# The first batch of a channel-attention and gated feed-forward kernel: ten groups of squares added up on VectorE, all norm products behind the scores, four filler products in place of fifty-six

## The chip, the cores and the metric

The kernel runs on one core of one Trainium2 chip. The metric is the device time of one execution in microseconds, over several executions of each kernel.

A profile shows one execution. PE is TensorE, PEld its weight loads, DVE VectorE, ACT ScalarE, POOL GpSimd.

## The reference, cut to what matters

```python
def _attn_ref(q, k, v, tau):                      # (4, 6016, 256) each
    qn = q / (np.linalg.norm(q, axis=1, keepdims=True) + 1e-06)
    kn = k / (np.linalg.norm(k, axis=1, keepdims=True) + 1e-06)
    s = kn.transpose(0, 2, 1) @ qn / tau          # 256 x 256 per batch
    a = softmax(s, axis=-1)                       # cut: written out with max, exp, sum
    return v @ a
def _moe_ref(x, w_gate, w_val, w_out):            # x: the attention's rows, d_ff 1536
    return (sigmoid(x @ w_gate) * (x @ w_val)) @ w_out
```

The norm runs over all 6016 rows, so nothing of a batch's attention can be finished before its last rows of q and k are there.

## The kernel before

The kernel folds `a` into the feed-forward weights, so the main loop multiplies v by folded weights (`gh_G`, `gh_H`) and then by `w_out`. For batches 1 to 3 the scores and norms are side work in the loop of the batch before. For batch 0 they stand in front of everything: the prologue. It works on groups of 4 x 128 rows, the last group being cut in two (groups 11 and 12).

```python
def score(b, t0, u):                 # per 128 rows: 2 products into the 256 x 256 scores
    ...
def squares(b, t0, nt, which, engine, sq=None):   # elementwise squares, q on VectorE, k on ScalarE
    # (the last group the other way round)
    ...
def norm_mms(ps, sqs, nt, first, last, order=(0, 1)):
    for w in order:                  # column sums of the squares: one product per 128 columns
        for u in range(nt):
            for j in range(CB):
                mm(ps[:, w*CB+j : w*CB+j+1], sqs[w][:, u, ds(j*P, P)], ones_bf[:, 0:1], ...)
def busy(n):                         # filler products that keep TensorE at work
    ps = psg.tile([P, CH], FP32, tag="g", name="ps_busy")
    for _ in range(n):
        mm(ps, ones_bf, ones_wide, True, True)    # 512 wide

busy(9)
n_acc = NT // TPC - 2                # 9 groups are added up on VectorE into acc
for g, (t0, nt) in enumerate(groups0):
    # squares; if 0 < g < n_acc: acc += sq (two additions on VectorE)
    # scores of the group
    if g < n_acc:          busy(5)
    elif g == n_acc:       norm_mms(acc); norm_mms(sq of group 9)
    elif nt == TPC:        busy(2); norm_mms(sq of group 10)
    elif g < last0:        held = (sq, nt)
    else:                  norm_mms(held); norm_mms(sq of group 12)
norms_sqrt(0)                        # ScalarE, then the table load for exp
...                                  # invert, spread, weights (exp), folded weights gh(0, 0..4)
```

## Time and profile before

| | before |
|---|---|
| median time | 830.18 us (829.69 to 830.32, 3 runs); 829.94 us with 3 more |
| span of the profiled execution | 827.9 us |
| PE busy | 817.6 us (99%) |
| first product of the main loop (ps_gate) | at 39.08 us |
| last k tile used by scores / square root of the norms / first weight product | 33.5 / 34.32 / 36.85 us |

From 40 us on, TensorE has almost no idle time (busy 19.95 of the 20 us to 60 us, and 739.3 of the 740 us from 60 to 800 us), so the end moves only if the first ps_gate product moves. In the timeline, a line gives start, length, engine, source line, operation and count. The bracket says how long the engine was idle before the line and what ended that.

### The profile page before, as it was taken

To read this page: it belongs to the slowest core of one execution; us is meant where nothing else is said; L and a number is where in the kernel's file an instruction comes from. 1 tells how busy PE (TensorE), PEld (TensorE's weight loads), DVE (VectorE), ACT (ScalarE), POOL (GpSimd) and SP (SyncE) were. 2 spreads that over 40 slices of the span, in tenths; PEclk is the share of its full clock that TensorE was granted. 3 is DMA by queue.
4 is the path that set the end of the run, shared out by engine and by line. 5 is a ranking of instruction groups with operands and counts; after the bars stand their busy time and mean duration, and the time that the engine had idled before them with its cause. 6 is when DMAs were issued, how large, how long until landed. Compare 5 with 4: busy or idle time off the path is not lost.

```text
span 827.9 us, 13794 instructions
## 1 busy us (share of the span) xinstructions
PE 817.6 (99%) x5204; PEld 503.5 (61%) x5218; DVE 588.7 (71%) x1023; ACT 391.7 (47%) x644; POOL 83.1 (10%) x159
## 2 busy tenths in 40 slices
PE   8899999999999999999999999999999999999998
PEld 4556666665665666665575666666566566666666
DVE  6577877787667777778767777777766666666665
ACT  4654444446644444445654444444655444444442
POOL 5532100002110100000311010000000000000000
PEclk9999999999999999999999999999999999999999
DMA  9999623226846433233875352223323423322111
GB/s 210 206 202 212 112 52 90 59 54 136 154 93 118 96 89 61 53 52 87 155 139 128 81 106 57 51 64 74 64 62 63 71 52 86 68 49 70 45 36 72
DMA packets 79027, 77.19 MB, mean 93 GB/s; under 512 B 50800, under 2 KB 55920, under 8 KB 78960
## 3 DMA queue, kind: packets, MB, share of 16 engines
q0 software_dynamic: 23920, 38.81, 28.1%
q1 hardware_dynamic: 54752, 36.91, 17.6%
q8 instruction: 41, 0.67, 0.3%
q10 hardware_dynamic: 288, 0.59, 0.2%
q14 instruction: 26, 0.21, 0.1%
HBM read 78.64 MB, written 24.64 MB: 125 GB/s over the span
## 4 chain that ended last, share of the span: by engine, by line
PE 94%; DMA 4%; DVE 1%; issue 0%; POOL 0%; ACT 0%; POOLq 0%
PE ps_o L88 30%; PE ps_gate L88 29%; PE ps_val L88 29%; PE ps_s L88 4%; DMA q_sb<-in_q_dram 3%; PE ps_gh L88 2%; DMA w_val<-in_moe_w_val_dram 1%; DVE hT L424 0%; DVE sq L176 0%; PE ps_end L88 0%; ACT g_sb L423 0%; PE ps_n L88 0%; POOL k_sb L97 0%; POOL q_sb L97 0%; PE ps_tp L394 0%
## 5 line engine op out<-in xcount | busy, mean ns | idle before, releaser
L424 DVE TENSOR_TENSOR hT<-ps_val,g_sb 128x512 bf16<-128x512 f32 (+1 forms) x576 | 390.7, 679 | 205.6 <-ACT g_sb L423 201.0
L423 ACT ACTIVATE g_sb<-ps_gate 128x512 bf16<-128x512 f32 (+1 forms) x576 | 338.3, 588 | 386.0 <-PE ps_gate L88 379.7
L88 PE MATMUL ps_gate<-vT,gh_G 128*128 128x512 bf16 (+1 forms) x1152 | 337.7, 375 | 0.2
L88 PE MATMUL ps_val<-vT,gh_H 128*128 128x512 bf16 (+1 forms) x1152 | 337.5, 375 | 0.3
L88 PE MATMUL ps_o<-w_out_sb,hT 128*128 128x256 bf16 x2244 | 324.9, 273 | 0.0
L88 PEld LDWEIGHTS <-hT 128*128 128x128 bf16 x2268 | 221.0, 98 | 124.6
L88 PEld LDWEIGHTS <-gh_H 128*128 128x128 bf16 x1152 | 112.7, 98 | 131.6 <-issue 1.0
L88 PEld LDWEIGHTS <-gh_G 128*128 128x128 bf16 x1152 | 112.4, 98 | 37.8 <-DVE gh_G L379 0.4
L106 POOL DMA_DIRECT2D v_sb<-in_v_dram x48 | 25.6, 533 | 619.7 <-DMA vT<-v_sb 498.5
L450 DVE COPY out_sb<-ps_o 128x256 f32<-128x256 f32 x187 | 77.2, 413 | 12.6 <-PE ps_o L88 12.6
L88 PE MATMUL ps_s<-k_sb,q_sb 128*128 128x256 bf16 x376 | 67.0, 276 | 3.9 <-DMA k_sb<-in_k_dram 2.7
L88 PEld LDWEIGHTS <-q_sb 128*128 128x128 bf16 x376 | 37.1, 99 | 12.7 <-issue 5.0
L215 DVE TENSOR_TENSOR acc<-acc,sq 128x1024 bf16<-128x1024 bf16 (+1 forms) x66 | 44.1, 669 | 0.0
L176 DVE TENSOR_TENSOR sq<-q_sb 128x1024 bf16<-128x1024 bf16 (+2 forms) x44 | 29.3, 667 | 2.7 <-DMA q_sb<-in_q_dram 2.7
L97 POOL DMA_DIRECT2D k_sb<-in_k_dram x48 | 26.2, 545 | 17.1 <-DMA k_sb<-in_k_dram 8.1
L97 POOL DMA_DIRECT2D q_sb<-in_q_dram x48 | 26.3, 548 | 14.9 <-DMA q_sb<-in_q_dram 7.4
L176 DVE TENSOR_TENSOR sq<-k_sb 128x1024 bf16<-128x1024 bf16 (+2 forms) x34 | 22.4, 658 | 0.9 <-ACT sq L174 0.9
L88 PE MATMUL ps_busy<-ones_wide,ones_bf 128*128 128x512 bf16 x57 | 17.7, 440 | 1.7 <-DVE shift L127 1.6
L174 ACT ACTIVATE sq<-k_sb 128x1024 bf16<-128x1024 bf16 (+1 forms) x11 | 11.2, 1018 | 14.5 <-DMA k_sb<-in_k_dram 13.1
L487 DVE TENSOR_TENSOR acc<-acc,sq 128x1024 bf16<-128x1024 bf16 x16 | 11.1, 691 | 5.5 <-ACT sq L174 5.2
L88 PE MATMUL ps_gh<-w_val,e_sb 128*128 128x512 bf16 x44 | 13.4, 379 | 0.2
L88 PEld LDWEIGHTS <-e_sb 128*128 128x128 bf16 x112 | 10.2, 98 | 4.7 <-ACT e_sb L311 0.5
(67 smaller groups left out, 133.8 us busy)
## 6 DMA issues: line engine op xcount, KB each, us to landing
out_dram<-out_sb SPq DMA_DIRECT2D x44, 512.0 KB, 2.9
v_sb<-in_v_dram POOLq DMA_DIRECT2D x44, 256.0 KB, 3.8
q_sb<-in_q_dram POOLq DMA_DIRECT2D x43, 256.0 KB, 7.3
k_sb<-in_k_dram POOLq DMA_DIRECT2D x43, 256.0 KB, 8.0
out_dram<-out_sb SPq DMA_DIRECT2D x3, 384.0 KB, 2.5
w_gate<-in_moe_w_gate_dram POOLq DMA_DIRECT2D x3, 256.0 KB, 6.8
w_val<-in_moe_w_val_dram POOLq DMA_DIRECT2D x3, 256.0 KB, 7.4
w_out_sb<-in_moe_w_out_dram POOLq DMA_DIRECT2D x1, 768.0 KB, 12.7
```

What stands on the lines that cost most here:

```text
L88: nc.tensor.matmul(out, lhsT=lhsT, rhs=rhs, start=start, stop=stop, **kw)
L97: nc.gpsimd.dma_start(out=tl[:, :nt, :], in_=rows(src, b)[:, t0 : t0 + nt, :])
L106: nc.gpsimd.dma_start(out=v_sb[:, :nt, :], in_=rows(v, b)[:, t0 : t0 + nt, :])
L174: nc.scalar.activation(out=sq[:, :nt, :], in_=src[:, :nt, :], func=ACT.Square)
L176: engine.tensor_tensor(out=sq[:, :nt, :], in0=src[:, :nt, :], in1=src[:, :nt, :], op=ALU.mult)
L215: nc.vector.tensor_tensor(out=acc[:, :nt, :], in0=acc[:, :nt, :], in1=st[b]["sq", w][:, :nt, :], op=ALU.add)
L423: nc.scalar.activation(out=g_sb[:, :n], in_=ps_gate[:, :n], func=ACT.Sigmoid)
L424: nc.vector.tensor_tensor(out=hts[b, ci][:, f, :n], in0=ps_val[:, :n], in1=g_sb[:, :n], op=ALU.mult)
L450: nc.vector.tensor_copy(out=out_sb[:, s, :], in_=ps)
L487: nc.vector.tensor_tensor(out=acc[w], in0=acc[w], in1=sq[w], op=ALU.add)
```

## The change

Its intent is to spend less TensorE work on the prologue. VectorE adds up one more group (60 norm products become 44), all norm products stand behind the last score, and 4 fillers remain of 56 (a few later ones stay as they are). In both diffs and code, `...` marks a cut.

```diff
-    sqpool = pool("sqpool", 2)
+    sqpool = pool("sqpool", 3)
...
-    busy(9)
-    n_acc = NT // TPC - 2
+    n_acc = NT // TPC - 1
+    parts = [(acc, TPC)]
     for g, (t0, nt) in enumerate(groups0):
...
+        elif g:
+            parts.append((sq, nt))
         for u in range(nt):
             score(0, t0, u)
-        if g < n_acc:
-            busy(5)
-        elif g == n_acc:
-            norm_mms(ps_n0, acc, TPC, True, False)
-            norm_mms(ps_n0, sq, nt, False, False)
-        elif nt == TPC:
-            busy(2)
-            norm_mms(ps_n0, sq, nt, False, False)
-        elif g < last0:
-            held = (sq, nt)
-        else:
-            norm_mms(ps_n0, *held, False, False)
-            norm_mms(ps_n0, sq, nt, False, True, (1, 0))
+        if n_acc - 3 <= g <= n_acc:
+            busy(1)
+    for n, (sq, nt) in enumerate(parts):
+        norm_mms(ps_n0, sq, nt, n == 0, n == len(parts) - 1, (1, 0) if n else (0, 1))
```

## The prediction

> **What bounds the kernel now.** I read the page first, then the chain in order of time for 26 to 41 us, then the timeline of the first 40 us. The change touches only the first batch's scores and norms, so the first question is what share of the span that is.
>
> ```profile
> span 827.9 us, 13794 instructions
> PE 817.6 (99%) x5204; PEld 503.5 (61%) x5218; DVE 588.7 (71%) x1023; ACT 391.7 (47%) x644; POOL 83.1 (10%) x159
> ```
>
> TensorE is busy for 99% of the span. The three big product groups (ps_gate, ps_val, ps_o) carry 88% of the chain, and the change touches none of them. Its only field is the prologue, about 39 us, before the first ps_gate product at 39.08. What bounds the prologue is in the chain:
>
> ```profile
> 19.61 10.58 DMA q_sb<-in_q_dram
> 30.19 0.28 issue
> 30.47 6.80 DMA w_val<-in_moe_w_val_dram
> 37.27 0.04 issue
> 37.31 0.59 PE ps_gh L88 x2
> ```
>
> From 3.46 to 37.27 us (start, length, what) nearly the whole chain is transfers: the loads of q and k, queued one after the other, then the first w_val tile. TensorE work there is not on it. The stretches say the same (PE, PEld, DVE, ACT, POOL busy, clock, DMA share, GB/s):
>
> ```profile
> 20.00:26.00 6.00, 4.73 (x28) 2.69 (x28) 4.92 (x8) 2.11 (x2) 2.25 (x5) 1.00 1.13 211
> 26.00:32.00 6.00, 4.44 (x58) 3.38 (x58) 2.28 (x4) 2.59 (x3) 2.75 (x5) 1.00 1.16 203
> ```
>
> The DMA share is above 1 and 203 to 211 GB/s flow, while PE has gaps. But one line of work runs beside the w_val transfer and ends almost with it. From the timeline:
>
> ```profile
> 33.19 0.82 PE L88 MATMUL ps_s<-k_sb,q_sb 128*128 128x256 bf16 x6
> 33.84 0.44 PE L88 MATMUL ps_n<-ones_bf,sq 128*128 128x1 bf16 x12
> 34.32 0.17 ACT L278 ACTIVATE r<-ps_n 128x4 f32<-128x4 f32 x1 [0.50 <-PE ps_n L88]
> 34.51 1.28 ACT L505 ACT_TABLE_LOAD   x1
> 35.88 1.65 ACT L311 ACTIVATE e_sb<-y_sb,shift,r 128x128 bf16<-128x128 f32 x4
> 36.85 0.38 PE L88 MATMUL ps_gh<-w_gate,e_sb 128*128 128x512 bf16 x1
> ```
>
> Read downwards: last scores, last 12 norm products, square root, table load, exponentials, first weight product at 36.85. That one holds PE for two 512-wide products of 0.215 us, so to 37.28; the next needs w_val, which landed at 37.27. So the **slack of the norm line is only about 0.03 us**: transfer and norm line end together. Whatever lengthens the norm line moves the end.
>
> [...] (1) [...]the 12 norm products start at 33.84 and the filler behind them at 34.15, 26 ns each; 16 from 32.79 to 33.19 are 25 ns each. (2) [...]512-wide fillers are 0.43 us apart up to 10.11 us, and 0.215 us apart later; 8 scores take 1.86 us at 6.74 and 1.03 us at 12.58. The profile's clock column shows 1.00 throughout, so this state has to be read from spacings. (3) [...]The trace has 1.28 us; [...]the exponential starts 0.09 us after the load. (4) [...]GpSimd's load issues take 0.53 us whether or not a VectorE product lies over them (12.14 us and 10.83 us), so more additions should not hold back the loads.
>
> **The change, part by part.**
>
> *Fillers.* The program issued 9 at the start, 5 after each of nine groups and 2 at group 10: 56. Four remain (groups 7 to 10). At 0.215 us each, 52 x 0.215 = 11 us of PE work goes (more, as the early ones ran at 0.43). Before about 33 us all of it lies beside transfers: from 22 us on, PE waits for k each time (idle of 0.42 to 1.21 us before scores). **Worth 0 us**, except that PE no longer lags behind arrivals before 20 us, which it had caught up with by then anyway.
>
> *One more group added up on VectorE.* Group 9 gets two additions of 0.691 us (the 16 present ones took 11.1 us). VectorE was busy 2.28 of 6.00 us from 26 to 32. The second addition follows ScalarE's square, which ends at 29.06 + 1.06 = 30.12, so it runs to 30.81; the q square of group 10 slips from 30.28 to 30.81 and ends at 31.50, before its k square (31.52 to 32.58). **Worth 0 us.** It saves 16 norm products: 60 become 44.
>
> *Three buffers for squares.* The squares of groups 10, 11 and 12 now all live until the end. With three buffers none waits. **0 us.**
>
> *Norm products behind the scores.* This is the part that costs. Before, 16 (acc) and 16 (group 9) ran in a gap near 29.9, 16 more at 32.79 before the scores of group 11, and only 12 stood behind the last score. Now all 44 stand there. The gain: the k of group 11 is in at about 32.89 (ScalarE's square starts), so its 4 scores no longer wait until 33.19; but group 12's 2 scores need its last k, in at about 33.46 (issued 26.96, 6.5 us to landing). So the scores are through at about 33.76, not 33.84: 0.08 us gained. The loss: 44 - 12 = 32 more products x 25.6 ns = 0.82 us. The last square is done at 33.82 and is multiplied last, so it adds nothing. Net: the square root starts 0.82 - 0.08 = **0.74 us later**.
>
> *Behind that.* The table load is queued after the square root, the exponentials after the load, so all of it shifts by 0.74 us. The copies of the scores on VectorE no longer matter, and the fillers in front of ps_rk run meanwhile. The first weight product goes from 36.85 to 37.59; w_val is then long in. After the 0.03 us of slack, **about +0.7 us** remains. Nothing later takes it back, as PE has hardly any idle time after 40 us (15.95 of 16 us busy from 44 to 60).
>
> Sum with the array at full rate at the end of the prologue: 830.18 + 0.7 = 830.9 us.
>
> **The rivals.** *A cold array.* With the fillers gone, PE starts cold at 6.74. Cold, 8 scores last about 1.7 us of a 2.5 us group period (68%). For: the kernel before only got fast after 10.11 us, although PE was busy from 1.60 with one gap of 1.14 us[...]. Warm, only 0.87 of 2.5 us is busy (35%), 1.09 with the filler. Against: groups 0 to 2 run nearly without a gap from 6.74 to about 12.3 when cold[...]; gaps afterwards are 1.5 us[...]; and the four fillers raise a cold array to 85% just before the end. If it is cold at 33 us: 6 scores + 0.4 us, 44 norm products perhaps + 1.1, the four fillers and ps_rk about + 1, the first weight products + 1; about 3.5 us on top, so 834.5 us. I give this one chance in four, some of it in milder form.
>
> *Hidden after all or a gain.* If the norm line had slack that I misread (w_val landing later in most runs than in the profiled one), the 0.7 us would be hidden: 830.2. If the earlier scores or the idler PE gained anything, it is at most a few tenths, as transfers set the pace: 829.9. One chance in six together.
>
> *VectorE or the loads slowed.* More additions holding up load issues would move every later landing. The trace speaks against it (4). One in twenty; about + 1 us.
>
> **Range and chances.** The likeliest value is 830.9, the cold tail pulls the median up a little: 831.1. Low end 829.9 (a small gain, near the fastest runs before), high end 834.2 (most of the cold case). 2% is 16.6 us; the whole prologue is 39 us and bound by transfers, so neither bound is in reach.
>
> **What would show it.** Right: the row of ps_n shows 44 products in one block of about 1.1 us starting near 33.8; the square root starts near 35.1; the first ps_gate near 39.8; the q, k and w_val landings unchanged within a few tenths; all after 40 us merely shifted. Cold: 8 scores near 1.7 us at groups 9 and 10, ps_gh products 0.43 us apart. Wrong: a square root that starts no later than 34.4, w_val landing later than 37.6, or a loop after 40 us that itself changed length.

0.82 - 0.08 - 0.03 is about +0.7 us, on 830.18 us, so 830.9 us. In (3), the 1.28 us are those of the table load. The rival of a cold array (834.5 us) is the estimate from the two rates in the trace of before; at how much work or idle time the rate changes was not shown.

## The result, and the profile after

The changed kernel takes 829.73 us (829.49 to 829.80, 6 runs), against 829.94 us (829.69 to 830.32, 6 runs) for the kernel before. The ratio is 0.9997 with a 95% interval of 0.9984 to 1.001: **the same**. Ratios here are the mean time of one kernel's fast runs over that of the other's of the same rounds, so they are not quite the ratio of the medians quoted. The forecast class was right. The forecast number was not: 829.73 lies just below the stated low end of 829.9, and the forecast direction (+0.7 us) did not come.

The page of the changed kernel, its busy row and the granted TensorE clock in 40 slices:

```profile
span 827.8 us, 13658 instructions
PE 810.3 (98%) x5138; PEld 500.3 (60%) x5150; DVE 590.4 (71%) x1025; ACT 391.7 (47%) x644; POOL 83.4 (10%) x159
PEclk8799999999999999999999999999999999999999
```

TensorE does 7.3 us less work and the span is the same (827.8 against 827.9 us), because that work stood beside transfers. The clock row begins with 8 and 7, so the array now runs at a lower rate in part of the prologue. ("Cold" below means at half rate: granted clock 0.50, 8 scores in 1.86 to 1.87 us. "Warm" means at full rate: 1.00, and 1.03 us.) By stretch (PE, PEld, DVE, ACT, POOL busy, then granted clock, DMA share, GB/s):

```profile
14.00:20.00 6.00, 3.68 (x20) 2.38 (x19) 4.43 (x7) 2.55 (x3) 2.42 (x6) 0.68 1.12 209
20.00:26.00 6.00, 4.10 (x19) 2.54 (x19) 4.92 (x9) 2.17 (x3) 2.53 (x5) 0.50 1.12 209
26.00:33.00 7.00, 6.02 (x32) 3.75 (x32) 4.31 (x8) 3.84 (x5) 4.32 (x7) 0.73 1.17 205
```

From 16.1 to 29.8 us the array was at half rate, and the transfers flowed as before (205 to 209 GB/s; 206 to 211 before, in the same stretches). The cold array cost nothing, as it was warm again before the last k (32.86 us). The end of the prologue in the timeline after, the same rows as the prediction shows of before:

```profile
32.23 1.05 PE L88 MATMUL ps_s<-k_sb,q_sb 128*128 128x256 bf16 x6
...
33.12 0.54 PE L88 MATMUL ps_n<-ones_bf,acc 128*128 128x1 bf16 x16
...
33.52 0.84 PE L88 MATMUL ps_n<-ones_bf,sq 128*128 128x1 bf16 x28
...
34.40 0.17 ACT L278 ACTIVATE r<-ps_n 128x4 f32<-128x4 f32 x1 [1.19 <-PE ps_n L88]
...
34.59 1.28 ACT L499 ACT_TABLE_LOAD   x1
...
36.92 0.38 PE L88 MATMUL ps_gh<-w_gate,e_sb 128*128 128x512 bf16 x1
```

The longer norm line is there. From the first product behind the last score to the square root it takes 34.40 - 33.12 = 1.28 us, against 34.32 - 33.84 = 0.48 us before: 0.80 us more, where 0.82 was predicted. But it **begins 0.72 us earlier**, at 33.12 rather than 33.84, where 0.08 was predicted. So the square root comes 0.08 us later (34.40: the prediction had named "no later than 34.4" as a sign of being wrong), and the first ps_gate at 39.13 instead of 39.08. The chain after confirms that the norm line is now on it, behind the last k:

```profile
26.38 6.48 DMA k_sb<-in_k_dram
32.87 0.04 issue
32.91 0.38 PE ps_s L88 x2
33.28 1.08 PE ps_n L88 x44
34.36 0.24 PE ps_busy L88
```

The last k is in at 26.38 + 6.48 = 32.86 us. Before, by its issue at 26.96 and 6.5 us to landing, it was in at about 33.46. Where does that 0.6 us come from? GpSimd's issues, which wait for earlier loads to land, show it. Before:

```profile
23.39 0.53 POOL L97 DMA_DIRECT2D k_sb<-in_k_dram  x1 [0.70 <-DMA k_sb<-in_k_dram]
24.89 0.53 POOL L97 DMA_DIRECT2D q_sb<-in_q_dram  x1 [0.97 <-DMA q_sb<-in_q_dram]
26.96 0.53 POOL L97 DMA_DIRECT2D k_sb<-in_k_dram  x1 [1.54 <-DMA k_sb<-in_k_dram]
28.03 0.53 POOL L106 DMA_DIRECT2D v_sb<-in_v_dram  x1 [0.54 <-DMA q_sb<-in_q_dram]
```

After:

```profile
23.66 0.53 POOL L97 DMA_DIRECT2D k_sb<-in_k_dram  x1 [0.70 <-DMA k_sb<-in_k_dram]
25.16 0.53 POOL L97 DMA_DIRECT2D q_sb<-in_q_dram  x1 [0.97 <-DMA q_sb<-in_q_dram]
26.38 0.53 POOL L97 DMA_DIRECT2D k_sb<-in_k_dram  x1 [0.69 <-DMA k_sb<-in_k_dram]
27.44 0.53 POOL L106 DMA_DIRECT2D v_sb<-in_v_dram  x1 [0.52 <-DMA q_sb<-in_q_dram]
```

One wait differs: 1.54 us instead of 0.69, a load that landed 0.85 us late in the kernel before. Everything else runs at the same pace; the changed kernel had been 0.27 us behind until then (23.66 against 23.39), which leaves the 0.58 us. The DMA view of that moment (24 to 25 us of before; queue, packets, MB, share of the 16 transfer engines) has a second queue in it:

```profile
q0 software_dynamic: 102, 0.19, 103.6%
q8 instruction: 1, 0.02, 6.1%
```

In the changed kernel the first such packet is at 34.5 us (34 to 35 us):

```profile
q0 software_dynamic: 203, 0.19, 118.0%
q8 instruction: 1, 0.02, 5.8%
```

The view names the kind of this queue "instruction", so I read its packets as fetches of instructions. The one at 24.1 us took 0.97 us (6.1% of 16 engines for 1 us), the one at 34.5 us 0.94 us. Each has 16,384 bytes, and the DMA view counts 41 of them (0.67 MB) before and 40 (0.66 MB) after. So the **theory**, mine and tested below: a change in the number of TensorE's instructions moves the packet in time. With 52 fillers and 16 norm products fewer (the page counts 5,138 products and 5,150 weight loads, against 5,204 and 5,218 before) it comes 10.4 us later, behind the last k instead of in front of it, and that gave back what the norm line cost.

The packet is not gone. At 34.5 us the w_val tiles are still on their way, and now they are late. The view of w_val gives the time from issue to landing of its three loads, before and then after:

```profile
DMA to landing us min/median/max: 6.8/7.4/8.7
DMA to landing us min/median/max: 7.3/8.0/9.1
```

The first of them is the shortest. It was issued 0.58 us earlier than before (29.89, not 30.47) and landed at 37.2 us, as before (37.27). In the traces of all thirteen profiles it landed between 37.1 and 37.5 us: in 6.8 us where no packet fell between its issue and its landing, in 7.3 to 7.6 us where one did. So moving the packet behind k shortens the norm line, but not the line through w_val.

### The profile page after: what moved, and what is told of

Same layout as the page of the kernel before. It is cut to its first block, busy times and chain, and to the rows that moved or that the text cites. A ratio compares the mean times of both kernels' runs of the same rounds, so it can differ in the third digit from the quotient of the medians.

```text
span 827.8 us, 13658 instructions
## 1 busy us (share of the span) xinstructions
PE 810.3 (98%) x5138; PEld 500.3 (60%) x5150; DVE 590.4 (71%) x1025; ACT 391.7 (47%) x644; POOL 83.4 (10%) x159
## 4 chain that ended last, share of the span: by engine, by line
PE 95%; DMA 3%; POOL 1%; DVE 1%; issue 0%; ACT 0%; POOLq 0%
PE ps_o L88 30%; PE ps_gate L88 29%; PE ps_val L88 29%; PE ps_s L88 4%; DMA k_sb<-in_k_dram 3%; PE ps_gh L88 2%; DVE hT L424 0%; POOL q_sb L97 0%; PE ps_n L88 0%; POOL k_sb L97 0%; DVE sq L176 0%; PE ps_end L88 0%; ACT g_sb L423 0%; ACT e_sb L311 0%; PE ps_busy L88 0%
## 5 line engine op out<-in xcount | busy, mean ns | idle before, releaser
L106 POOL DMA_DIRECT2D v_sb<-in_v_dram x48 | 25.6, 533 | 620.5 <-DMA vT<-v_sb 487.5
L88 PE MATMUL ps_s<-k_sb,q_sb 128*128 128x256 bf16 x376 | 73.1, 298 | 13.2 <-ACT k_sb L130 7.0
L88 PEld LDWEIGHTS <-q_sb 128*128 128x128 bf16 x376 | 40.0, 106 | 23.6 <-issue 8.9
L88 PE MATMUL ps_gh<-w_gate,e_sb 128*128 128x512 bf16 x41 | 12.8, 379 | 0.2
```

The source lines that it names most:

```text
L88: nc.tensor.matmul(out, lhsT=lhsT, rhs=rhs, start=start, stop=stop, **kw)
L106: nc.gpsimd.dma_start(out=v_sb[:, :nt, :], in_=rows(v, b)[:, t0 : t0 + nt, :])
```

## The experiments

Rivals: the early k is chance (B), or the missing fillers' work itself lets the loads run faster (C).

**The kernel before once more** (no edit).

> The kernel before, unchanged, for a second profile. Theory A (instruction fetch): [...]this profile too shows one instruction packet between 23.5 and 25 us, the issue of group 12's k load at about 26.9 us instead of about 26.4, and that k (and group 12's scores) in at about 33.5. Theory B (a chance delay of one load in the one profiled run): no such gap in this one, issues every 1.2 us up to v, last k in at about 32.9, and the first ps_gate product at about 38.5 rather than 39.1.

The packet came at 24.3 us, the k issue at 27.19, the last scores from 33.42, the square root at 34.55 and ps_gate at 39.30. The single time was 830.39 us. The late load repeats (and does so a third time in norms_only below), so B falls.

**Padding in front of the changed kernel.**

```diff
+    ps_pad = psg.tile([P, CH], FP32, tag="g", name="ps_pad")
+    for _ in range(50):
+        mm(ps_pad[:, 0:1], ones_bf, ones_wide[:, 0:1], True, True)
     ps_n0 = psm.tile([P, 2 * CB], FP32, tag="m", name="ps_n")
```

> The changed kernel with 50 one-column products (100 TensorE instructions) put in front, in the idle time before the first k arrives at 7 us. Theory A (instruction fetch): [...]the first instruction packet moves from 34.5 back to about 24 us, the last k lands about 0.6 us later than in the changed kernel (33.5, not 32.9), and as the long norm line now follows it, the time is about 0.6 us over the changed kernel: ratio to before about 1.0006 (830.4). Theory C (it is the missing fillers' PE work that lets the loads run faster): the padding is nearly no work, so the last k stays at 32.9 and the time at that of the changed kernel, ratio 0.9997.

830.66 us (830.38 to 830.74), ratio 1.0007. The packet came at 19.4 us and not at 24, so my estimate of its moment was off. The issue that waited for the load behind it is plain:

```profile
21.84 0.53 POOL L97 DMA_DIRECT2D k_sb<-in_k_dram  x1 [1.56 <-DMA k_sb<-in_k_dram]
```

The norm products then start at 33.68 (changed kernel: 33.12) and ps_gate at 39.69. All five runs lie above every run of the changed kernel, in this study 829.49 to 829.90 over 16 runs (ten of them on other chips, the chip of the first six is not on record; before had 829.98 on this chip, 829.56 to 830.99). The padding is 1.5 us of work in idle time and does not delay the scores (first score at 6.90 us, changed kernel 6.99), so C, which needs the fillers' work, falls for this delay.

**The norm part alone.** The changed kernel with the fillers of before:

```diff
+    busy(9)
...
-        if n_acc - 3 <= g <= n_acc:
-            busy(1)
+        if g < n_acc - 1:
+            busy(5)
+        elif g == n_acc:
+            busy(2)
```

> The kernel before with ten groups added up and all 44 norm products behind the scores, but with its own 56 fillers. Theory A (instruction fetch): packet at 24 us as before, last k at 33.5, and 32 more products behind it: first ps_gate about 39.8, time + 0.7 us over before (ratio 1.0008), which is what the prediction's sum said of this part. Theory C (fillers slow the loads): the same. A rival in which the norm line is not on the path: ratio 1.0000.

830.52 us (830.36 to 831.9) against 829.98 of before: +0.54. Packet at 24.1, square root at 35.12, ps_gate at 39.84. That is 0.76 us behind the first profile of before (39.08), and 0.54 us behind the second, which is from this chip (39.30). This is the prediction's sum, measured, within the spread of two profiles: with the packet where it was, the norm line costs about the 0.7 us that was worked out.

**The filler part alone.** The kernel before with four fillers:

```diff
-    busy(9)
...
-        if g < n_acc:
-            busy(5)
+        if g in (7, 8, 9, 10):
+            busy(1)
+        if g < n_acc:
+            pass
...
-            busy(2)
```

> The kernel before with its norm products where they were, but with four fillers in place of 56. Theory A (instruction fetch): [...]the packet falls at 30 to 31.5 us, still ahead of the last k, which lands about as late as before (33.3 to 33.6): time within 0.2 us of before (ratio 1.0000). Theory C (the fillers' work slows the loads): last k at 32.9, norm line short, gain 0.5 us or more (ratio 0.9993 or less).

830.25 us (830.22 to 831.19), +0.27. The packet moved to 31.8 us, still in front of the last k, and that k now came late:

```profile
32.98 0.60 PE L88 MATMUL ps_s<-k_sb,q_sb 128*128 128x256 bf16 x4
34.10 0.38 PE L88 MATMUL ps_s<-k_sb,q_sb 128*128 128x256 bf16 x2 [0.52 <-DMA k_sb<-in_k_dram]
```

The two scores of group 12 wait for it until 34.10. So neither part gains alone: the two cost 0.54 and 0.27 us, and together they come out level. That is no sum of two effects. It is one packet that falls in front of or behind a landing.

The next four ran together on another chip, where before had 829.78 us (829.53 to 831.2, 9 runs).

**The changed kernel again.**

> The changed kernel, unchanged, on the chip and beside the runs of the next three. Theory A (instruction fetch): the first instruction packet again behind the last k (near 34.5 us), that k in at about 32.9, first ps_gate near 39.1, time 0.1 to 0.4 us under before. If the early landing was chance: packet or landing elsewhere, time 0.5 us or more over before.

829.81 us (829.52 to 829.90), ratio 0.9998. Packet at 34.4, norm products from 32.91, ps_gate at 39.09. The time is level with before here, not 0.1 to 0.4 us under it.

**A larger dose of padding** (`range(180)` in place of `range(50)`).

> The dose: 180 one-column products in front in place of 50[...]. Theory A: two instruction packets of about 0.95 us fall into the load-bound stretch before 33 us in place of one, each costing about as much as the one of after_pad did (0.6 to 0.9 us): last k near 34.2, first ps_gate near 40.4, time 0.6 to 0.9 us over after_pad and 1.4 to 1.7 us over before. Rival: only the first packet, or one at an unlucky place, costs anything: time as after_pad (830.7). A third: the padding itself delays the scores; then the scores of groups 9 to 11 would no longer wait for k.

830.54 us (830.3 to 830.83), ratio 1.0008. Packets came at 7.5 and 20.1 us, norm products from 33.90, ps_gate at 39.91. Against after_pad, which ran on the other chip, the second packet added 0.22 us to the start of the norm products, not 0.6 to 0.9, and nothing to the time, so this expectation of my own theory failed.

**Norm products in the gaps.**

```diff
+        if g >= n_acc and g < last0:
+            n = g - n_acc
+            norm_mms(ps_n0, *parts[n], n == 0, False, (1, 0) if n else (0, 1))
-    for n, (sq, nt) in enumerate(parts):
-        norm_mms(ps_n0, sq, nt, n == 0, n == len(parts) - 1, (1, 0) if n else (0, 1))
+    for n in (2, 3):
+        norm_mms(ps_n0, *parts[n], False, n == 3, (1, 0))
```

> The changed kernel with its norm products laid into the gaps between the scores again: those of acc after group 10's scores, group 10's after group 11's, 12 left behind the last. With the packet behind the last k (near 33.5 us; if it comes before 32.9 the gain is lost), the square root starts near 33.6 us, 0.8 us earlier than in the changed kernel. The w_val tile, in at about 37.2, then becomes the bound, so only 0.1 to 0.3 us are gained over the changed kernel: ratio to before about 0.9995. If w_val is not the bound: 0.8 us gained, ratio 0.9988.

829.80 us (829.66 to 829.97), as the changed kernel. The packet came at 34.4 and the square root at 33.91, 0.27 us earlier and not 0.8, as group 12's scores had to wait for group 10's products. Then a new wait appears:

```profile
37.50 0.59 PE L88 MATMUL ps_gh<-w_val,e_sb 128*128 128x512 bf16 x2 [0.32 <-DMA w_val<-in_moe_w_val_dram]
```

What the norm line gains, w_val takes: it landed 7.6 us after its issue, at 37.5 us, with the packet in between, and the first ps_gate is at 39.28. Two lines end together here, so shortening one alone is worth nothing.

**Without the four fillers.**

```diff
-        if n_acc - 3 <= g <= n_acc:
-            busy(1)
```

> The changed kernel without its four fillers. What the prediction's rival of a cold array said: cold scores keep TensorE busy for 1.7 of 2.5 us[...], so scores of group 10 take 1.7 us rather than 0.87, and norm products, ps_rk and the first weight products run at half rate: 2 to 4 us more, ratio to before 1.003 to 1.005. If the scores and norm products alone bring the clock back in time: within 0.5 us of the changed kernel. The granted clock column should show 0.5 up to 33 us or beyond in the first case.

830.18 us, but spread from 829.50 to 830.59. The profiled run was the slowest. Its array was at half rate from 30.6 to 34.0 us, and the last scores are cold:

```profile
30.80 3.15 PE L88 MATMUL ps_s<-k_sb,q_sb 128*128 128x256 bf16 x14 [1.41 <-DMA k_sb<-in_k_dram]
```

Its square root is at 35.08, 0.9 us behind that of the changed kernel on the same chip (34.18). Neither forecast fits: the cold tail exists, but costs about 0.8 us in the runs it hits, not 2 to 4. I take the two shortest runs (829.50, 829.79) for those that were warm in time: their mean granted clock was 0.994 and 0.993, that of the other three 0.990 to 0.992. Only the slow one was profiled.

The last three ran on a third chip, where before had 829.78 us (829.60 to 831.31).

**The changed kernel, third time.**

> The changed kernel once more, as the measure on this chip for the next two: packet near 34.4 us, last k in at about 32.8, 0.1 to 0.3 us under before.

829.58 us (829.57 to 829.86), ratio 0.9996. Packet at 34.1, norm products from 32.86, ps_gate at 38.90.

**One early packet** (`range(97)`).

> The changed kernel with 97 one-column products in front (194 TensorE instructions): by what the 50 and the 180 showed, the first packet should come at 4 to 8 us and the second only after about 33 us, so that one early packet lies in the load-bound stretch. Reading 1 (a packet costs the same wherever it falls there, and a second one on top costs less): the last k comes 0.4 to 0.7 us later than in the changed kernel, time 0.4 to 0.7 us over it. Reading 2 (an early packet is made up for by the loads behind it, only a late one costs): last k as in the changed kernel, time within 0.2 us of it.

830.44 us (830.3 to 831.46), 0.86 us over the changed kernel. There was one packet at 7.3 us and the next only at 37.7. Its mark is on the issue

```profile
9.62 0.53 POOL L97 DMA_DIRECT2D k_sb<-in_k_dram  x1 [1.90 <-DMA k_sb<-in_k_dram]
```

and the norm products start at 33.80, 0.94 us behind. So the first reading holds: a packet 25 us ahead of the last k costs as much as one shortly before it. The loads behind it did not make it up.

**Three packets** (`range(308)`).

> The changed kernel with 308 one-column products in front[...]: three packets ahead of the last k, near 5, 8 and 18 us. If packets add up: last k 1.5 us or more behind the changed kernel's, time 1.4 us or more over it. If they do not add up[...]: last k 0.6 to 0.9 us later, as with the 180, time 0.6 to 0.9 us over the changed kernel.

830.46 us (830.43 to 830.56). Packets came at 7.3, 13.3 and 20.0 us, norm products from 33.78, ps_gate at 39.79: the same as with one. Packets do not add up here. In this run TensorE itself stopped in the padding, for 1.81 us in which it waited for nothing that the profile shows:

```profile
1.59 6.09 PE L88 MATMUL ps_pad<-ones_wide,ones_bf 128*128 128x1 bf16 x223 [1.59 <-DVE shift L127]
9.49 2.41 PE L88 MATMUL ps_pad<-ones_wide,ones_bf 128*128 128x1 bf16 x85 [1.81 <-issue]
```

The first packet (7.3 us) begins just before that gap (7.68 to 9.49 us); what stopped TensorE was not shown. Its scores began only at 11.76 us and had caught up by 19.08, where they waited for k again. With these 616 instructions more, the DMA view counts 42 packets where the changed kernel has 40.

Together, in order of the landing that matters (the k of group 11 is read from the start of its square on ScalarE):

| run | packets before 33 us | k of group 11 | square root | first ps_gate | median us |
|---|---|---|---|---|---|
| after_third | none | 32.04 | 34.14 | 38.90 | 829.58 |
| after_again | none | 32.08 | 34.18 | 39.09 | 829.81 |
| after | none | 32.27 | 34.40 | 39.13 | 829.73 |
| between | none | 32.28 | 33.91 | 39.28 | 829.80 |
| no_fill | none | 32.21 | 35.08 | 39.81 | 830.18 |
| fillers_only | 31.8 | 32.16 | 34.82 | 39.55 | 830.25 |
| after_pad | 19.4 | 32.84 | 34.96 | 39.69 | 830.66 |
| before | 24.1 | 32.89 | 34.32 | 39.08 | 829.94 |
| pad_early | 7.3 | 32.95 | 35.08 | 39.81 | 830.44 |
| after_pad3 | 7.3, 13.3, 20.0 | 32.95 | 35.06 | 39.79 | 830.46 |
| norms_only | 24.1 | 33.02 | 35.12 | 39.84 | 830.52 |
| after_pad2 | 7.5, 20.1 | 33.06 | 35.17 | 39.91 | 830.54 |
| before_again | 24.3 | 33.12 | 34.55 | 39.30 | 830.39 (1 run) |

Without a packet early enough, the k of group 11 is in at 32.0 to 32.3 us; with one, two or three it is in at 32.8 to 33.1. In fillers_only the packet came too late for that k and delayed the next.

**What stays open.** (1) Why two or three packets cost no more than one (norm products from 33.78 to 33.90 us with each dose of 97, 180 and 308): measured, but its cause was not shown. (2) What sets the moment of a packet: counted in the traces, TensorE had between 195 and 292 records behind it when the first packet came without heavy padding, but 203, 369 and 429 with 97, 180 and 308 products in front, and there the packet came at 7.3 to 7.5 us each time. The count alone does not set it. That a packet in front of the last k delays it is shown by the padded runs whatever sets the moment. (3) No version clearly beat both kernels. By the 2% rule all of them are "the same", and the runs of norms_only and fillers_only overlap those of before (829.56 to 830.99); the times inside the traces carry the argument. The changed kernel and `between` are within 0.05 us of before on one chip. The first w_val tile, in at 37.1 to 37.5 us in every run, leaves little to win.

## Why the prediction was right or wrong, point by point

- **Fillers worth 0 us:** right for the work itself (7.3 us less busy time, same span), wrong for what else they are. Their number moves the moment of the packet: 24.1 us before, 31.8 us in fillers_only, 34.5 us after, and 19.4 us with 50 narrow products in front of the changed kernel.
- **One more group on VectorE, three buffers:** right, 0 us. GpSimd's issues of q and k kept their 0.53 us from 7 to 27 us. One reading under (4) was wrong: the issue at 10.83 us is no case without VectorE work, as an addition (10.51 to 11.20) lies over it. One with VectorE idle is at 26.96 us, also 0.53 us, so the conclusion stands. These issues show no wait for the additions.
- **Norm products:** the 32 more products were right: 0.80 us measured, 0.82 predicted, and 0.54 to 0.76 us at the first ps_gate where the packet stayed put (norms_only). The step that failed is "group 12's 2 scores need its last k, in at about 33.46", with the criterion "the q, k and w_val landings unchanged within a few tenths". The last k was in at 32.86, while w_val was in at 37.2 as forecast. The sum lacked one term: an instruction packet that moves from in front of the last k to behind it, about -0.6 us in the two profiled runs (0.6 to 0.9 us between the padded kernels and the changed one). That this term nearly cancels the longer norm line (0.80 us) is luck.
- **Slack of 0.03 us on the norm line:** right in kind. When `between` shortened the norm line, w_val became the wait (0.32 us).
- **A cold array:** right that it gets cold (half rate from 16.1 to 29.8 us), right that the four fillers speak against a cold end (full rate from 29.8 us with them in the changed kernel, from 34.0 us without them in no_fill, as profiled), too dear by four times in the one cold end that was profiled. There, without the fillers, it cost 0.9 us at the square root, not 3.5 us in all; the array was warm again at 34.0 us. The norm products do not slow as I had guessed: 97 narrow products in front (pad_early, from 1.60 us, when the fillers of before were still 0.43 us apart) took 2.73 us, 28 ns each, hardly more than the 25.6 ns of the warm ones. What sets the moment of a change of rate was not shown: in the three profiles of the changed kernel, the first slow scores behind warm ones start at 15.87, 15.65 and 13.15 us.
- **"The profile's clock column shows 1.00 throughout":** true of that profile, but I drew too much from it. In the changed kernel it reads 0.50 from 20 to 26 us, where 8 scores took 1.86 to 1.87 us. In the kernel before it reads 1.00 at 6.74 us too, where 8 scores took 1.86 us instead of 1.03.
- **"Hidden after all or a gain", low end 829.9:** the low end allowed 0.3 us of gain for the unknown. A second profile of before would have shown a repeated late load, and the DMA view of that microsecond its cause. I had neither.
- **Faster, same, slower:** same, as forecast, since 2% (16.6 us) was out of reach. This bears little on the mechanism.

## What to carry to other kernels

Here, where 203 to 211 GB/s flowed while TensorE had gaps, taking TensorE instructions away moved a packet of 16,384 bytes on the instruction queue from 24.1 to 34.5 us, and a packet in front of the last k was worth 0.6 to 0.9 us of its landing. So look at the instruction queue in the DMA view, and see which landing its packets fall in front of, before taking work beside transfers for free. The packet that left k fell on w_val (6.8 us to landing before, 7.3 after). When a change alters instruction counts, an effect of some tenths of a microsecond may come from this shift. Padding with cheap instructions (28 ns each here) helps to tell it apart, though a large dose can go along with a stop of the engine itself (1.81 us with 308 of them). Where two lines end together (norms and w_val here), work out both before shortening one.
